# Seven block products for eight: h2 of two token tiles at a time, and a fixed TensorE order in pairs

## The chip, the cores and the metric

The kernel runs on one core of one Trainium2 chip. The metric is device microseconds of one launch. Three runs of the kernel before gave 898.53 us as their median (897.16 to 900.41).

## The reference

Three layers follow each other on 3072 tokens (4 batches of 768). Retention attention gives x (3072 x 512). A first expert part gives y = (h - tanh h) w_out with h = x w_in (inner width 2048). The second expert part, with inner width 1024, is where the change lies:

```python
h = x @ w_in
e = np.exp(h - np.max(h, axis=-1, keepdims=True))
sm = e / (np.sum(e, axis=-1, keepdims=True) + 1e-09)
solu = h * sm
mu = np.mean(solu, axis=-1, keepdims=True)
var = np.mean((solu - mu) ** 2, axis=-1, keepdims=True)
ln = (solu - mu) / np.sqrt(var + 1e-06) * g_ln
return (ln @ w_out).astype(np.float32)
```

Here x is the first part's y. The weights of both parts come as float64 words and are decoded on the chip.

## The kernel before, in words

Engines are named as in the profile: PE is TensorE, DVE is VectorE, ACT is ScalarE, POOL is GpSimd, SP issues most DMAs. A product of two fp32 matrices is made of three matmuls: each operand is split into a high and a low part (a copy to fp32r on ACT, and a subtraction), and high x high, high x low and low x high are added up in PSUM.

The attention is followed by the first expert part, in six column blocks s of 512 tokens. For each f of 16 slices of the inner width, `products_h` (L337) makes 12 matmuls of 128x512 into a PSUM bank, `less_tanh` takes tanh (ACT, L344) and subtracts (DVE, L345), `split` makes the two parts (L350 to L353), and `products_y` (L362) makes 12 matmuls, two f behind. During the last block (s = 5) the weights of the second part are prepared beside this: `dec2.step` loads a weight tile, decodes it (ACT L126, four DVE instructions L133 to L140), scales it if it belongs to `w_out2` (ACT L148) and splits it (ACT L149, DVE L150). That makes 16 weight tiles, 8 of `w_in2` and 8 of `w_out2`. The first y tiles are reloaded from DRAM and split there too (`load_y`, `split_y`: SP L389, ACT L396, POOL L397).

The second part goes over 24 tiles of 128 tokens. `h2(i)` makes 24 matmuls (two halves of 512 columns, four slices of the inner dimension, three matmuls each, L568) into two PSUM banks, then the row maximum (DVE L574), the exponential with its sum (ACT L577), the product h times e with its sum (DVE L579), the subtraction of the mean (DVE L582, result u), the sum of squares (ACT L584) and small instructions that give the scale sc (DVE, POOL L591, L592). `trans(i)` transposes u by 8 matmuls of 128x128 (PE L603) into two PSUM banks, and splits the result (ACT L605, DVE L606). `outp(i)` makes 24 matmuls (L616) and writes the output tile (ACT L619, DMA L621). In the loop, trans runs one tile behind h2, and outp two.

The order of each engine's instructions is found by the framework's scheduler when the kernel is built, from a model of durations. It places instructions of different steps between each other. At run time each engine keeps its order strictly, and waits where an operand is not ready. Buffers come from two pools: `t4` with 44 buffers of 4 KB a partition, and `t2` with 15 of 2 KB.

The change replaces `h2`, `load_y`, `split_y`, the `w_in2` half of `dec2`, and the loop around them.

Of the kernel before, what the change touches and what calls it, by code (L numbers as in the profile page):

```python
# [90 lines left out]
def body(ctx: ExitStack, tc, z, w_in, w_out, w_in2, w_out2, g_ln, cst, tab, out):  # L91
# [274 lines left out]
    def keep_y(s, py):  # L366
# [14 lines left out]
        [w_in2[i] for i in range(NF2)] + [w_out2[i] for i in range(NF2)],  # L381
        [None] * NF2 + [gl[:, i : i + 1] for i in range(NF2)],
        nc.vector,
    )
    yl, ys = {}, {}

    def load_y(i):
        t = t2([P, NK, P], F32, "yl")
        nc.sync.dma_start(out=t, in_=y1d[i // B][:, i % B, :, :])  # L389
        yl[i] = t  # L390

    def split_y(i):
        t = yl.pop(i)
        y = t4([P, 2, NK, P], F32R, "y")
        yh, yo = y[:, 0, :, :], y[:, 1, :, :]
        nc.scalar.copy(yh, t)  # L396
        nc.gpsimd.tensor_tensor(yo, t, yh.bitcast(F32), ALU.subtract)  # L397
        ys[i] = (yh, yo)
# [126 lines left out]
    for n, (s, f) in enumerate(steps):  # L525
# [11 lines left out]
        if s == NSB - 1:  # L537
            if f < NF1 - 3:
                dec2.step()
            if f in (4, 7, 10):  # L540
                dec2.step()
            if f == NF1 - 6:
                load_y(0)
                load_y(1)
            if f == NF1 - 4:
                split_y(0)
# [6 lines left out]
    ps_2 = ctx.enter_context(tc.tile_pool(name="ps_2", bufs=2, space=PSUM, reuse_waits="tile"))  # L553
# [4 lines left out]
    uc, ut, sc2 = {}, {}, {}  # L558

    def h2(i):  # L560
        yh, yo = ys.pop(i)
        ph = ps_2.tile([P, 2, 512], F32, tag="h2", name="ph2")
        for half in range(2):
            n = 0
            for k in range(NK):
                bh, bl = dec2.w[2 * k + half]
                for a, b in ((yh, bh), (yh, bl), (yo, bh)):
                    nc.tensor.matmul(  # L568
                        ph[:, half, :], a[:, k, :], b, start=n == 0, stop=n == 3 * NK - 1
                    )  # L570
                    n += 1
        phf = ph.rearrange("p a b -> p (a b)")
        nmx = sp.tile([P, 1], F32, tag="nmx", name="nmx")
        nc.vector.tensor_reduce(nmx, phf, AX.X, ALU.max, negate=True)  # L574
# [117 lines left out]
```

## Time and profile before

| what | value |
|---|---|
| median of three runs | 898.53 us |
| the profiled execution's own time, as the span from its first to its last instruction | 899.2 us |
| mean granted TensorE clock over the span | 0.988 of full speed |
| busy share of the span: PE, DVE, ACT, POOL | 97%, 48%, 34%, 22% |
| matmuls | 6656 |
| instructions on DVE, ACT, POOL | 873, 606, 200 |

The busy share counts time in which an instruction ran on that engine. Matmuls overlap, so their single durations (some 0.39 us) are longer than the distance at which they follow each other; the pace is read from the starts. In the rows below, "idle before" in square brackets is the time for which the engine stood still ahead of an instruction, and what ended it.

### The profile page before, as it was taken

Reading aid. Unit: us, or ns where it says so; the run is one execution under the profiler, and the core shown is the slowest. Engines: PE = TensorE matmul, PEld = TensorE weight load, DVE = VectorE, ACT = ScalarE, POOL = GpSimd, SP = SyncE. Lnnn points to the kernel's source line nnn. Section 1 sums busy time; section 2 is a strip of 40 time slices with the busy share of each in tenths; the row PEclk is TensorE's granted clock in tenths of the full one; section 3 lists DMA queues with packets and bytes.
Section 4 is the critical chain, followed back from the end, with each engine's and each line's share of the span. In section 5 each row is a group of like instructions: output and inputs, shape, how many; then the busy total and the mean of one; then the engine's idle time right before and its main releaser. Section 6 shows DMA issues by size and latency. Waiting matters only on the chain.

```text
span 899.2 us, 15890 instructions
## 1 busy us (share of the span) xinstructions
PE 874.1 (97%) x6656; PEld 723.5 (80%) x6656; DVE 434.1 (48%) x873; ACT 301.4 (34%) x606; POOL 193.8 (22%) x200
## 2 busy tenths in 40 slices
PE   4699999999999999999999999999999999999998
PEld 4588888888888887888788888888888888888886
DVE  3679759981232232222222279954444444444442
ACT  4556436550111111111111134523444433333332
POOL 4411000000234333333333200011222212122210
PEclk8799999999999999999999999999999999999999
DMA  9663105340321112111310055114111111100000
GB/s 359 251 265 130 48 1 187 95 140 0 94 95 48 60 64 79 48 47 48 95 48 14 12 183 150 43 41 123 47 48 40 35 44 47 36 24 24 24 24 35
DMA packets 34775, 71.93 MB, mean 80 GB/s; under 512 B 3088, under 2 KB 15504, under 8 KB 34704
## 3 DMA queue, kind: packets, MB, share of 16 engines
q1 hardware_dynamic: 18288, 58.01, 19.0%
q10 hardware_dynamic: 16416, 12.91, 4.5%
q8 instruction: 52, 0.85, 0.4%
q14 instruction: 19, 0.16, 0.1%
HBM read 58.32 MB, written 12.58 MB: 79 GB/s over the span
## 4 chain that ended last, share of the span: by engine, by line
PE 94%; DMA 2%; issue 1%; DVE 1%; ACT 1%; POOL 1%; ACTq 0%; POOLq 0%
PE ph L337 29%; PE py L362 29%; PE po L616 15%; PE ph L568 15%; PE out L211 3%; PE ptr L603 2%; PE sc L211 2%; DMA z<-z 1%; DMA con<-cst 1%; DMA y1d<-ysb 0%; POOL qs L223 0%; POOL vs L234 0%; DVE g L345 0%; ACT th L344 0%; DVE w L150 0%
## 5 line engine op out<-in xcount | busy, mean ns | idle before, releaser
L362 PE MATMUL py<-gh,w 128*128 128x512 f32 x768 | 248.8, 392 | 0.0
L337 PE MATMUL ph<-xh,w 128*128 128x512 f32 x768 | 247.9, 393 | 0.0
L337 PEld LDWEIGHTS ph<-xh,w 128*128 128x128 f32 x768 | 145.3, 189 | 31.0
L362 PEld LDWEIGHTS py<-gh,w 128*128 128x128 f32 x768 | 143.3, 188 | 30.4 <-ACT gh L350 0.2
L345 DVE TENSOR_TENSOR g<-ph,th 128x512 f32<-128x512 f32 x96 | 66.2, 690 | 182.3 <-ACT th L344 182.3
L337 PE MATMUL ph<-xl,w 128*128 128x512 f32 x384 | 150.4, 392 | 0.0
L362 PE MATMUL py<-gl,w 128*128 128x512 f32 x384 | 149.8, 390 | 0.0
L344 ACT ACTIVATE th<-ph 128x512 f32<-128x512 f32 x96 | 57.3, 598 | 258.9 <-PE ph L337 245.9
L568 PE MATMUL ph<-w,y 128*128 128x512 f32 x576 | 134.9, 389 | 0.0
L353 POOL TENSOR_TENSOR gl<-g,gh 128x512 fp32r<-128x512 f32 x48 | 61.9, 1289 | 331.6 <-DVE gh L352 298.0
L568 PEld LDWEIGHTS ph<-w,y 128*128 128x128 f32 x576 | 108.0, 188 | 22.4
L616 PE MATMUL po<-w,uh 128*128 128x512 f32 x384 | 120.4, 395 | 0.0
L397 POOL TENSOR_TENSOR y<-yl,y 128x512 fp32r<-128x512 f32 x24 | 42.2, 1761 | 260.9 <-ACT y L396 260.9
L574 DVE TENSOR_REDUCE nmx<-ph 128x1 f32<-128x1024 f32 x24 | 29.4, 1225 | 117.7 <-PE ph L568 117.7
L337 PEld LDWEIGHTS ph<-xl,w 128*128 128x128 f32 x384 | 72.6, 189 | 14.9
L362 PEld LDWEIGHTS py<-gl,w 128*128 128x128 f32 x384 | 72.1, 188 | 14.9
L616 PEld LDWEIGHTS po<-w,uh 128*128 128x128 f32 x384 | 70.6, 188 | 13.6
L616 PE MATMUL po<-w,ul 128*128 128x512 f32 x192 | 75.3, 392 | 0.0
L577 ACT ACTIVATE ex<-ph,nmx 128x1024 f32<-128x1024 f32 x24 | 26.8, 1117 | 132.5 <-DVE nmx L574 132.5
L579 DVE SCALAR_TENSOR_TENSOR ex<-ph,ex 128x1024 f32<-128x1024 f32 x24 | 29.4, 1225 | 29.8 <-ACT ex L577 29.8
L616 PEld LDWEIGHTS po<-w,ul 128*128 128x128 f32 x192 | 36.0, 188 | 7.6
L353 DVE TENSOR_TENSOR gl<-g,gh 128x512 fp32r<-128x512 f32 x48 | 33.8, 707 | 10.1 <-PE py L362 8.1
(76 smaller groups left out, 840.4 us busy)
## 6 DMA issues: line engine op xcount, KB each, us to landing
z<-z SPq DMA_DIRECT2D x48, 512.0 KB, 5.3
raw<-w_in SPq DMA_DIRECT2D x24, 512.0 KB, 5.2
raw<-w_out SPq DMA_DIRECT2D x24, 512.0 KB, 3.7
y1d<-ysb ACTq DMA_DIRECT2D x24, 256.0 KB, 3.5
yl<-y1d SPq DMA_DIRECT2D x24, 256.0 KB, 3.2
out<-ob ACTq DMA_DIRECT2D x24, 256.0 KB, 2.2
tab<-tab SPq DMA_DIRECT2D x5, 256.0 KB, 2.6
tab<-tab ACTq DMA_DIRECT2D x1, 256.0 KB, 4.7
```

Of the source, the lines that this page charges most:

```text
L211: pin(nc.tensor.matmul(o, a, b, start=True, stop=True, skip_group_check=True))
L337: nc.tensor.matmul(ph, a[:, k, :], x, start=n == 0, stop=n == 3 * NK - 1), s < 2
L344: nc.scalar.activation(th, ph, AF.Tanh)
L345: nc.vector.tensor_tensor(g, ph, th, ALU.subtract)
L353: eng_l.tensor_tensor(gl_, g, gh.bitcast(F32), ALU.subtract)
L362: nc.tensor.matmul(py[e], a[:, cols], x, start=f == 0 and n == 0, stop=f == NF1 - 1 and n == 2)
L397: nc.gpsimd.tensor_tensor(yo, t, yh.bitcast(F32), ALU.subtract)
L568: nc.tensor.matmul(ph[:, half, :], a[:, k, :], b, start=n == 0, stop=n == 3 * NK - 1)
L574: nc.vector.tensor_reduce(nmx, phf, AX.X, ALU.max, negate=True)
L577: nc.scalar.activation(ex, phf, AF.Exp, bias=nmx, scale=1.0, accum_out=ssum)
L579: nc.vector.scalar_tensor_tensor(ex, phf, 1.0, ex, ALU.mult, ALU.mult, accum_out=us)
L616: nc.tensor.matmul(po, a[:, f, :], b, start=n == 0, stop=n == 3 * NF2 - 1)
```

## The change

The product of two token tiles with `w_in2` is taken as a 2 by 2 block product. The blocks of the left matrix are A11, A12 (the first tile, first and second half of the 512 inner columns) and A21, A22 (the second tile); the blocks of the right one are B11, B12, B21, B22 (256 inner rows by 512 columns). It is made of seven block products instead of eight: P1 = A11 B11, P2 = A12 B21, and P3 to P7 with sums of blocks on both sides. Each block product is six matmuls (two inner slices, three matmuls each), so a pair takes 42 matmuls for 48.

The weights' side is made once, during the last block of the first part: `Combined` decodes the 8 tiles, forms three sums and one difference a slice on POOL (`combine`, 8 instructions of 128x512 in all) and splits 14 tiles instead of 8. The tokens' side is made for each pair: `split_y(j)` loads two tiles by one DMA, forms four sums on POOL (128x256 each), and splits seven blocks instead of four by three ACT casts (512, 256 and 1024 elements) and three POOL subtractions of the same sizes.

On the output side the PSUM banks of partial results are read and accumulated in steps: P1 is copied out (`keep`, ACT), P6 is accumulated on the same bank and copied out, then P7, copied out again. `add_half` (DVE, one instruction with a running minimum, and a read of it) adds a bank and a copy into `hn` in SBUF and gives the negated maximum, four times a pair. The row maximum of before is gone, and `soft` takes its input from SBUF.

TensorE's order in the second part is the program's order (`manual_schedule`), in pairs; the other engines' order is still the scheduler's.

```diff
+        def combine(self, r):
+            b12, b11, b22, b21 = (self.wf.pop(4 * r + i) for i in range(4))
+            t1, t2_, t4_ = (t2([P, 512], F32, "wf") for _ in range(3))
+            nc.gpsimd.tensor_tensor(t1, b12, b11, sub)
...
+        nc.gpsimd.tensor_tensor(s1, a21, a22, ALU.add)
+        nc.gpsimd.tensor_tensor(s2, s1, a11, ALU.subtract)
+        nc.gpsimd.tensor_tensor(s3, a11, a21, ALU.subtract)
+        nc.gpsimd.tensor_tensor(s4, a12, s2, ALU.subtract)
...
+            nc.scalar.copy(h, src)
+            nc.gpsimd.tensor_tensor(o, src, h.bitcast(F32), ALU.subtract)
...
-            if f < NF1 - 3:
-                dec2.step()
-            if f in (4, 7, 10):
+            if f < 12:
+                com.step()
+            if f >= 8:
                 dec2.step()
...
+    def keep(ph):
+        t = t2([P, 512], F32, "part")
+        nc.scalar.copy(t, ph)
+        return t
...
+        nc.vector.tensor_tensor_reduce(
+            hn[:, half * 512 : (half + 1) * 512], ph, part, -1.0,
+            3.0e38 if seen is None else nm[seen], ALU.add, ALU.min, nm[half],
+        )
...
+    with tc.manual_schedule(engines={mybir.EngineType.PE}):
+        for j in range(NJ + 1):
...
+            if now:
+                h_a, h_b = new_h(), new_h()
+                q1, q2 = bank(), bank()
+                product(j, P1, q1)
+                part1 = keep(q1)
+                product(j, P2, q2)
+                add_half(h_b, 0, q2, part1, None)
+            if was:
+                trans(a)
+            if now:
+                product(j, P6, q1, False)
+                part2 = keep(q1)
+                q3 = bank()
+                product(j, P5, q3)
+            if was:
+                trans(b)
+            if now:
+                product(j, P7, q1, False)
+                part3 = keep(q1)
+                add_half(h_a, 1, q3, part3, None)
+            if was:
+                outp(a, range(4))
+            if now:
+                q4 = bank()
+                product(j, P4, q4)
+                add_half(h_a, 0, q4, part3, 1)
+                soft(2 * j + 1, h_a, 0)
+                product(j, P3, q3, False)
+                add_half(h_b, 1, q3, part2, 0)
+                soft(2 * j, h_b, 1)
+                ys.pop(j)
+            if was:
+                outp(a, range(4, NF2))
+                outp(b, range(NF2))
```

In a pair, a is the second tile and b the first. The new lines that the prediction speaks of are L457 to L460 (sums of a pair, POOL), L468 and L469 (its splits, ACT and POOL), L642 (block products), L649 (keep), L657 (add_half), L667 to L673 (soft), L692 to L695 (trans), L706 (outp) and L712 (the output copy).

Three places show what moved. The first is ACT in the middle of the second part. Before, for one tile (`y` is the split tile, `u` the centred tile, `ob` the output tile):

```order
L577 ACTIVATE ex,ssum<-ph_6738,nmx 128x1024
L605 CAST uh<-ptr 128x512 x2
L396 CAST y<-yl 128x512
L584 ACTIVATE ex,ssq<-u 128x1024
L619 ACTIVATE ob<-po,sc 128x512
L621 DMA out<-ob 128x512
```

Now, for one pair, from its exponentials to the first copy (`part`) of the next pair and the casts of the transposed tiles (`yha` and `yhs` are the high parts of the pair after next):

```order
L667 ACTIVATE ex,ssum<-hn,nm 128x1024 x2
L468 CAST yha<-yl 128x512
L468 CAST yha<-yl 128x256
L712 ACTIVATE ob<-po,sc 128x512
L714 DMA out<-ob 128x512
L673 ACTIVATE ex,ssq<-hn 128x1024 x2
L468 CAST yhs<-ysum 128x1024
L712 ACTIVATE ob<-po,sc 128x512
L714 DMA out<-ob 128x512
L649 COPY part<-ph_6730 128x512
L694 CAST uh<-ptr 128x512 x2
L649 COPY part<-ph_6730 128x512
```

The copies that free a bank for the next accumulation stand behind both sums of squares, a cast and an output copy of the pair before.

The second place is PE where the second part starts. Before, h2 of the second tile is followed by a part of the third, and then by the first transposes (`u_6192` is the first tile's):

```order
L568 MATMUL ph2_6208<-w_5471,y_6154 128x512 x3
L568 MATMUL ph2_6208<-w_5563,y_6154 128x512 x3
L568 MATMUL ph2_6208<-w_5618,y_6154 128x512 x3
L568 MATMUL ph2_6208<-w_5706,y_6154 128x512 x3
L568 MATMUL ph2_6273<-w_5415,y_6203 128x512 x2
L603 MATMUL ptr_6254<-ident_6150,u_6192 128x128 x4
L603 MATMUL ptr_6261<-ident_6150,u_6192 128x128 x4
L568 MATMUL ph2_6273<-w_5415,y_6203 128x512
```

Now the last block product of the first pair (P3, on `ph2_6246`) is followed by P1 and P2 of the second pair, and then by the transposes of tile a of the first (`hn_6215`):

```order
L642 MATMUL ph2_6246<-w_5941,yhs_6004 128x512 x2
L642 MATMUL ph2_6246<-w_5941,yls_6005 128x512
L642 MATMUL ph2_6332<-w_5594,yha_6199 128x512 x2
L642 MATMUL ph2_6332<-w_5594,yla_6200 128x512
L642 MATMUL ph2_6332<-w_5774,yha_6199 128x512 x2
L642 MATMUL ph2_6332<-w_5774,yla_6200 128x512
L642 MATMUL ph2_6333<-w_5597,yha_6199 128x512 x2
L642 MATMUL ph2_6333<-w_5597,yla_6200 128x512
L642 MATMUL ph2_6333<-w_5777,yha_6199 128x512 x2
L642 MATMUL ph2_6333<-w_5777,yla_6200 128x512
L692 MATMUL ptr_6351<-ident_6192,hn_6215 128x128 x4
L692 MATMUL ptr_6358<-ident_6192,hn_6215 128x128 x4
```

Between the end of a tile's h2 and its transposes stood 26 matmuls; now 18 stand between P4, the last product that tile a needs, and its transposes.

The third place is PE at the end. Before, the last tile's transposes (`u_8250`) stand between the matmuls of the output product of the tile before it:

```order
L616 MATMUL po_8321<-w_5897,uh_8261 128x512 x2
L603 MATMUL ptr_8314<-ident_6150,u_8250 128x128 x4
L616 MATMUL po_8321<-w_5897,ul_8262 128x512
L616 MATMUL po_8321<-w_5909,uh_8261 128x512 x2
L616 MATMUL po_8321<-w_5909,ul_8262 128x512
```

Now the transposes of both last tiles stand behind each other, with no matmul between:

```order
L706 MATMUL po_8451<-w_6135,uh_8351 128x512 x2
L706 MATMUL po_8451<-w_6135,ul_8352 128x512
L692 MATMUL ptr_8481<-ident_6192,hn_8297 128x128 x4
L692 MATMUL ptr_8488<-ident_6192,hn_8297 128x128 x4
L692 MATMUL ptr_8497<-ident_6192,hn_8300 128x128 x4
L692 MATMUL ptr_8504<-ident_6192,hn_8300 128x128 x4
L706 MATMUL po_8511<-w_5800,uh_8479 128x512 x2
```

There are two PSUM banks for transposed halves, so the third group of four waits until the first bank has been read.

## Rows read from the trace of the kernel before

**Rows 1.** The page's chain that ended last, by engine and by line.

```profile
PE 94%; DMA 2%; issue 1%; DVE 1%; ACT 1%; POOL 1%; ACTq 0%; POOLq 0%
PE ph L337 29%; PE py L362 29%; PE po L616 15%; PE ph L568 15%; PE out L211 3%; PE ptr L603 2%; PE sc L211 2%; DMA z<-z 1%; DMA con<-cst 1%; DMA y1d<-ysb 0%; POOL qs L223 0%; POOL vs L234 0%; DVE g L345 0%; ACT th L344 0%; DVE w L150 0%
```

**Rows 2.** Busy time by stage (us of PE, PEld, DVE, ACT, POOL, then clock, DMA).

```profile
540.00:560.00 20.00, 20.00 (x90) 16.57 (x89) 19.35 (x40) 7.68 (x13) 0.00 (x0) 1.00 0.52 160
...
700.00:800.00 100.00, 100.00 (x479) 83.55 (x478) 44.70 (x97) 39.67 (x70) 22.14 (x25) 1.00 0.12 38
```

**Rows 3.** Timeline of PE, one tile of the second part (start us, us).

```profile
647.38 5.61 PE L568 MATMUL ph<-w,y 128*128 128x512 f32 x24
652.83 1.03 PE L603 MATMUL ptr<-ident,u 128*128 128x128 f32 x8
653.62 0.71 PE L616 MATMUL po<-w,uh 128*128 128x512 f32 x2
...
659.15 1.07 PE L568 MATMUL ph<-w,y 128*128 128x512 f32 x4
```

**Rows 4.** Groups by line and form, 640 to 860 us (busy us, mean ns of one).

```profile
L606 DVE TENSOR_TENSOR ul<-ptr,uh 128x512 fp32r<-128x512 f32 x38 | 24.4, 682 | 0.0
...
L605 ACT CAST uh<-ptr 128x512 fp32r<-128x512 f32 x38 | 20.2, 588 | 0.0
L584 ACT ACTIVATE ex<-u 128x1024 f32<-128x1024 f32 x19 | 20.2, 1063 | 15.1 <-DVE u L582 15.1
...
L582 DVE TENSOR_SCALAR u<-ex,us 128x1024 f32<-128x1024 f32 x19 | 14.3, 753 | 0.0
L619 ACT ACTIVATE ob<-po,sc 128x512 f32<-128x512 f32 x19 | 13.1, 688 | 9.7 <-PE po L616 9.7
```

**Rows 5.** One line's instructions on POOL (ns: min/median/max), 256 and 512 elements.

```profile
L324 POOL TENSOR_TENSOR xl<-xf,xh x31: 724/732/794, 20.1 to 516.7; 128x256 fp32r<-128x256 f32 x31
...
L397 POOL TENSOR_TENSOR y<-yl,y x24: 1296/1839/1850, 589.4 to 857.5; 128x512 fp32r<-128x512 f32 x24
```

**Rows 6.** Timeline of DVE and ACT, one tile's softmax: where each hop starts.

```profile
700.18 1.23 DVE L574 TENSOR_REDUCE nmx<-ph 128x1 f32<-128x1024 f32 x1 [5.41 <-PE ph L568]
...
702.68 1.23 DVE L579 SCALAR_TENSOR_TENSOR ex<-ph,ex 128x1024 f32<-128x1024 f32 x1 [1.27 <-ACT ex L577]
...
704.14 0.75 DVE L582 TENSOR_SCALAR u<-ex,us 128x1024 f32<-128x1024 f32 x1
...
701.44 1.12 ACT L577 ACTIVATE ex<-ph,nmx 128x1024 f32<-128x1024 f32 x1 [5.96 <-DVE nmx L574]
```

**Rows 7.** Timeline where POOL and DVE meet, 589 and 704 us.

```profile
589.38 2.80 POOL L397 TENSOR_TENSOR y<-yl,y 128x512 fp32r<-128x512 f32 x2 [66.42 <-ACT y L396]
589.51 1.52 DVE L352 CAST gh<-g 128x512 fp32r<-128x512 f32 x1
...
704.21 1.85 POOL L397 TENSOR_TENSOR y<-yl,y 128x512 fp32r<-128x512 f32 x1 [8.53 <-ACT y L396]
```

**Rows 8.** Timeline of PE and ACT where the second part starts.

```profile
612.86 10.59 PE L568 MATMUL ph<-w,y 128*128 128x512 f32 x46
...
612.93 0.59 ACT L372 COPY ysb<-py 128x512 f32<-128x512 f32 x1 [0.65 <-DVE ysb L370]
```

**Rows 9.** Timeline of PE and ACT at the end.

```profile
883.64 0.60 PE L603 MATMUL ptr<-ident,u 128*128 128x128 f32 x4
...
894.80 0.39 PE L616 MATMUL po<-w,ul 128*128 128x512 f32 x1
895.28 0.69 ACT L619 ACTIVATE ob<-po,sc 128x512 f32<-128x512 f32 x1 [4.75 <-PE po L616]
```

**Rows 10.** PE in the attention part: a gap, and the clock after it.

```profile
41.95 0.37 PE L211 MATMUL out<-vq,sa 64*64 64x64 f32 x2 [3.87 <-issue]
...
45.00:50.00 5.00, 5.00 (x76) 3.85 (x75) 1.12 (x3) 1.54 (x4) 2.02 (x2) 0.68 1.03 412
```

More of the change, by code (lines that the diff above doesn't have):

```diff
@@ L380, in body @@
     dec2 = Decoder(
-        [w_in2[i] for i in range(NF2)] + [w_out2[i] for i in range(NF2)],
-        [None] * NF2 + [gl[:, i : i + 1] for i in range(NF2)],
-        nc.vector,
-    )
-    yl, ys = {}, {}
[L387 to L398, printed above, removed]
+        [w_out2[i] for i in range(NF2)], [gl[:, i : i + 1] for i in range(NF2)], nc.vector
+    )
@@ L552, in body @@
     sp = ctx.enter_context(tc.tile_pool(name="sp", bufs=3))
-    ps_2 = ctx.enter_context(tc.tile_pool(name="ps_2", bufs=2, space=PSUM, reuse_waits="tile"))
+    ps_2 = ctx.enter_context(tc.tile_pool(name="ps_2", bufs=4, space=PSUM, reuse_waits="tile"))
     ps_t = ctx.enter_context(tc.tile_pool(name="ps_t", bufs=2, space=PSUM, reuse_waits="tile"))
@@ L557, in body @@
     nc.sync.dma_start(out=ident, in_=cst[:, C_IDENT:])
[L558 to L574, printed above, removed]
+    uc, ut, sc2, po_of = {}, {}, {}, {}
@@ new lines, in bank, with product @@
+    def bank():
+        return ps_2.tile([P, 512], F32, tag="h2", name="ph2")
+    def product(j, m, ph, first=True):
+        a = ys[j][m]
+        n = 0
+        for r in range(2):
+            bh, bl = com.w[m, r]
+            for x, w in ((a[0], bh), (a[0], bl), (a[1], bh)):
+                nc.tensor.matmul(
+                    ph, x[:, r, :], w, start=first and n == 0, stop=n == 5, skip_group_check=True
+                )
+                n += 1
+    def keep(ph):
+        t = t2([P, 512], F32, "part")
+        nc.scalar.copy(t, ph)
+        return t
@@ L575, in h2, with new_h, add_half, soft @@
+    def new_h():
+        return t4([P, FF2], F32, "hn"), [sp.tile([P, 1], F32, tag=f"nm{i}", name="nm") for i in range(2)]
+    def add_half(h, half, ph, part, seen):
+        hn, nm = h
+        nc.vector.tensor_tensor_reduce(
+            hn[:, half * 512 : (half + 1) * 512], ph, part, -1.0,
+            3.0e38 if seen is None else nm[seen], ALU.add, ALU.min, nm[half],
+        )
+    def soft(i, h, last):
+        hn, nmx = h[0], h[1][last]
         ex = t4([P, FF2], F32, "ex")
         ssum = sp.tile([P, 1], F32, tag="ssum", name="ssum")
-        nc.scalar.activation(ex, phf, AF.Exp, bias=nmx, scale=1.0, accum_out=ssum)
+        nc.scalar.activation(ex, hn, AF.Exp, bias=nmx, scale=-1.0, accum_out=ssum)
@@ L592, in h2 @@
         nc.gpsimd.tensor_tensor(sc, sc, ssum, ALU.mult)
-        uc[i], sc2[i] = u, sc
+        uc[i], sc2[i] = hn, sc
     def trans(i):
@@ L607, in trans, with outp @@
         ut[i] = (uh, ul)
-    def outp(i):
-        uh, ul = ut.pop(i)
-        po = ps_o.tile([P, DM], F32, tag="o", name="po")
-        n = 0
-        for f in range(NF2):
-            bh, bl = dec2.w[NF2 + f]
-            for a, b in ((uh, bh), (uh, bl), (ul, bh)):
-                nc.tensor.matmul(po, a[:, f, :], b, start=n == 0, stop=n == 3 * NF2 - 1)
-                n += 1
+    def outp(i, fs):
+        uh, ul = ut[i]
+        if fs[0] == 0:
+            po_of[i] = ps_o.tile([P, DM], F32, tag="o", name="po")
+        po = po_of[i]
+        for f in fs:
+            bh, bl = dec2.w[f]
+            for n, (a, b) in enumerate(((uh, bh), (uh, bl), (ul, bh))):
+                nc.tensor.matmul(
+                    po, a[:, f, :], b, start=f == 0 and n == 0, stop=f == NF2 - 1 and n == 2
+                )
+        if fs[-1] < NF2 - 1:
+            return
         ob = t2([P, DM], F32, "ob")
```

101 lines of the change are left out of this document (81 added, 20 removed).

## The prediction

> **What bounds the kernel now.** I read the chain of waits first: PE is 94% of it, and the second part's two matmul lines, L568 and L616, are 15% of the span each [rows 1]. Then busy time by stage: from 700 to 800 us PE is busy throughout at full clock, DVE for 45%, ACT for 40%, POOL for 22% [rows 2]. So the second part is bound by PE alone, and there removed matmuls shorten the span one for one, as long as PE's fixed order never waits. The timeline of one tile gives the pace: 24 matmuls of h2 take 652.83 - 647.38 = 5.45 us, 0.227 each; the transposes take 0.79; the output product 5.53 [rows 3]. All times below are against the profiled execution's span, 899.2 us; the median of the runs is 0.67 below it, and I take that off at the end. 0.3% (2.7 us) is about what a measurement of this kernel can tell from no change.
>
> **What goes.** 576 matmuls of h2 become 504: 72 x 0.227 = **16.35 us**. Their shape stays, 128x512, so the pace does. The transposes and the output product are the same in number.
>
> **What is added, in the middle of the second part.** All of it lies on engines that idle for more than half of this stage; the question is whether PE's order meets a result that is late. I follow one pair from the end of P4 (0). PE then has P3 (1.36), 36 output matmuls (8.18, to 9.54), P1 and P2 of the next pair (to 12.27), the transposes of a (to 13.06), and P6, which must wait for the copy of P1's bank. Hops are from the trace: PE to a reader 0.25 (the last matmul starts at 894.80, its reader at 895.28, less 0.23) [rows 9]; exponential to product 1.24, product start to centring start 1.46 with its small instructions [rows 6].
> - `add_half` is in no row. Bounds: 0.68 (DVE, 512 elements, one operand in PSUM, L606 [rows 4]) and 1.23 (the reduction of 1024 [rows 6]). I take 0.7, as its size is L606's.
> - So tile a has its maximum at 1.05, exponential to 2.2, product to 3.5; tile b's product runs from 3.65 to 4.9; centring a to 6.0, b to 6.8; squares (1.06 each, L584, and 0.1 for a hop) to 7.2 and 8.35; the cast yhs of 1024 elements (taken as the square's 1.06 [rows 4]) to 9.4; the output copy of b, 0.69, to 10.5, as its product ends at 9.54; the copy of P1's bank (0.59, L605) follows P1's end at 10.9 and is done at 11.8. P6 is due at 13.06. Spare: 1.2 us, and the late part of the chain (the cast's end) could slip by 2.2.
> - The transposes of a need centring a (6.0) at 12.27. P7 needs P6's copy: done 0.84 after P6, with P5 and a transpose (2.15) in between. P3 needs P7's copy and an `add_half`, 1.6 after P7, with 12 output matmuls and P4 (4.1) as cover. None waits.
> - POOL: 256 elements take 0.73, 512 take 1.29 alone [rows 5]; 1024 are in no row, 2.4 by these two. A pair has 5 x 0.73 + 1.29 + 2.4 = 7.35 us for 22, and is split a whole pair ahead. The two `yla` subtractions and the last sum fall behind the cast of `yha`, that is at 4.4, into DVE's chain.
>
> There the two engines meet. A DVE cast of 0.43 that started 0.13 after a POOL instruction took 1.52, and POOL's subtraction of 1.29 took 1.85 when DVE's centring had started just before [rows 7]: whichever was second stood still. So each of DVE's three big instructions there can be held by one POOL instruction: centring b moves from 6.8 to 8.3, the cast's end from 9.4 to 10.5, the copy's hardly at all. Still no wait on PE. The Trainium skill (SBUF — State Buffer, section Who interferes with whom) states it as an exclusive lock, taken for a whole instruction, between GpSimd and a DVE instruction with two SBUF inputs or in a two-port mode. By that rule this change adds to it, because L669 now reads both inputs from SBUF, where L579 had one in PSUM; the trace agrees for the cast (1.52 for 0.43). By the rows' three instructions the sum below stands; by the rule at its strictest, with every POOL instruction of the pair in DVE's way, it would be rival 1's.
>
> **Where PE does wait: the first pair.** Nothing of an earlier pair covers it, and before nothing waited there: 46 matmuls run from 612.86 without a gap [rows 8]. In time after the last y product of the first part (612.86):
> - P1's rest and P2 end at 1.8. P1's copy stands on ACT behind the y copies (to 613.52 [rows 8]) and the 1024 cast of the second pair: done at 0.66 + 1.06 + 0.59 = 2.3, with the hop to PE 2.5. **0.7.**
> - P3 needs 1.6 + 0.1 after P7, covered by P4 alone (1.36). **0.35.**
> - The transposes of a: from P7's end, copy 0.84, two `add_half` 1.4, exponential 1.3, the products of a and b 2.5, small instructions and hops 0.8, centring 0.75: 7.6. PE has P4, P3, P1 and P2 of the second pair and the wait before: 5.8. So 1.8, and 3.1 if one POOL subtraction of 1.29 is in front. I take **2.5.**
> - The transposes of b need the banks of a's. ACT's order in this one pair puts a's casts behind both squares, the 1024 cast and P6's copy: from centring a, 1.1 + 1.2 + 1.1 + 0.6 + 1.2 for the casts + 0.7 + 0.1 for the last subtraction = 6.0; PE has transposes, P6 and P5, 3.5, and the halves overlap by 0.3. **2.2.**
>
> Sum 5.8. Bounds: 4 if POOL is never in front, 8 if `add_half` takes 1.23 and POOL is in front twice.
>
> **And at the end.** Before, the last transposes lie between output matmuls [rows 9]. Now four groups of four stand together on two banks: output copy 0.94, casts 0.59 twice, subtractions to 2.85, the last group to 3.35, where 1.58 would do: **1.8** (bounds 1 and 2.5).
>
> **In the last block of the first part** DVE gets 6 more splits of 0.68 (L606's form), 4.1 us, and POOL 8 instructions of 1.29. DVE is at 19.35 of 20 us there [rows 2], but y products run two f behind, some 10.9 us, and the decoding of `w_out2` moves to where DVE is idle. I cost it at nothing; the cover is that lag.
>
> **Sum:** -16.35 + 5.8 + 1.8 = -8.75: span 890.45, time **889.8**.
>
> **Rivals.**
> 1. *POOL holds DVE for longer* (slower than before). Place: between centring and the cast yhs of each pair. The cast's end at 9.4 may slip by 2.2 for nothing; behind that each us is paid 11 times; the gain is gone at 3.0. If the 1024 subtraction falls in as well, each holding DVE as in [rows 7], it is held for 1.29 + 2 x 0.73 + 2.4 = 5.15: 2.95 x 11 = 32 us, time 922. Against: the order puts that subtraction behind the pair's scale, so after the squares. 7%.
> 2. *`add_half` takes 1.23.* Then the chain is 1.1 longer a pair, with POOL's delay just at its spare, and the first pair pays 1.1 more: 891 to 897, as waits of 0 to 0.5 a pair come in. 11%.
> 3. *The clock falls in the first pair's gaps.* After a gap of 3.87 us the granted clock was 0.68 of 2.4 GHz, a mix of its levels 1.2 and 2.4, for the next stretch [rows 10]. Mine are 2 to 3 us. Some 10 us at two thirds cost 3.5: time 893.3. 9%.
> 4. *DVE is late in the last block of the first part.* If POOL's 8 instructions hold it for their 10.3 us on top of 4.1, and 6 of these are not covered: 896. 6%.
> 5. *The scheduler's order is kept better than I think and the first pair costs under 3 us:* time under 887, at the least 898.5 - 16.35 = 882. 5%.
>
> **Numbers.** Forecast 62%, its own range 886 to 893 by the bounds of the first pair and the end. Range 884.5 to 896.5: forecast, rivals 3 and 5 for the most part, 2 but its end, and half of 4. Faster (under 895.8): forecast 62, rival 2 most 8, rival 3 9, rival 5 5, less 2 for unknown waits, 82%; slower (over 901.2): rival 1 and 1 for the unknown, 8%; same 10%.
>
> **What would show it.** Right: 6584 matmuls; the second part's pairs 22.1 us apart with no gap of PE; some 6 us of PE's idle time within 25 us behind the first P1, put down to ACT or DVE, and 2 us before the last two output products. Wrong: a wait at L642 or L692 in every pair (then the chain through L673, L468 and L649 is longer than 13 us), L657 over 1 us, PE waiting at L362 between 520 and 612 us, or a clock under 1.0 after 612 us.

## The result, and the profile after

The changed kernel takes **890.09 us** (median of 4 runs, 889.34 to 890.77) beside 898.72 for the kernel before (897.16 to 900.41): a ratio of 0.9895, with a 95% interval of 0.9874 to 0.9917. The prediction was 889.8. A second set of runs gave 892.03, a ratio of 0.9912 (0.9898 to 0.9927).

The profiled execution's span is 889.0 us against 899.2. Its page begins like this (busy us, share of the span, instructions), and its chain that ended last reads, against [rows 1]:

```profile
PE 859.5 (97%) x6584; PEld 709.5 (80%) x6584; DVE 464.2 (52%) x951; ACT 335.1 (38%) x660; POOL 278.9 (31%) x268
...
PE 83%; DVE 8%; DMA 3%; issue 2%; ACT 1%; POOL 1%; ACTq 0%; POOLq 0%; DVEq 0%; SPq 0%
```

The 72 matmuls are gone (6656 to 6584), and DVE has come into the chain, with 8%. Busy time by stage, against [rows 2]:

```profile
700.00:800.00 100.00, 100.00 (x477) 83.41 (x476) 53.45 (x130) 52.02 (x90) 41.27 (x45) 1.00 0.13 48
```

The second part is still bound by PE alone: 100 of 100 us at full clock, while POOL's load has nearly doubled (22.14 to 41.27). What PE waited for behind the attention part, in the list of waits (us in total, times, longest):

```profile
PE ptr L692 <- DVE us L670: 2.3, 1, 2.3
PE ptr L692 <- DVE ul L695: 2.3, 2, 1.2
...
PE py L362 <- DVE gh L352: 1.1, 1, 1.1
...
PE ph L642 <- ACT part L649: 0.3, 1, 0.3
```

Four of these five waits are of the second part: three in the first pair, one at the end. The other, at L362, lies in the last block of the first part. PE's timeline has them in brackets:

```profile
601.63 0.39 PE L337 MATMUL ph<-xh,w 128*128 128x512 f32 x1
...
605.84 1.19 PE L362 MATMUL py<-gh,w 128*128 128x512 f32 x4 [1.11 <-DVE gh L352]
...
612.62 0.39 PE L642 MATMUL ph<-w,yha 128*128 128x512 f32 x1
...
614.92 0.73 PE L642 MATMUL ph<-w,yhs 128*128 128x512 f32 x2 [0.32 <-ACT part L649]
...
620.71 0.73 PE L642 MATMUL ph<-w,yhs 128*128 128x512 f32 x2
...
627.42 1.09 PE L692 MATMUL ptr<-ident,hn 128*128 128x128 f32 x8 [2.34 <-DVE us L670]
632.43 1.26 PE L692 MATMUL ptr<-ident,hn 128*128 128x128 f32 x8 [1.15 <-DVE ul L695]
...
870.74 1.03 PE L692 MATMUL ptr<-ident,hn 128*128 128x128 f32 x8
872.93 1.25 PE L692 MATMUL ptr<-ident,hn 128*128 128x128 f32 x8 [1.16 <-DVE ul L695]
873.94 0.70 PE L706 MATMUL po<-w,uh 128*128 128x512 f32 x2
```

What a wait costs is more than its bracket, since PE also has to run its pipeline empty and fill it again. So I count from start to start, at 0.227 a matmul and 0.79 for eight transposes [rows 3]: 0.48 before P6 (at 614.92), 0.34 before P3 (620.71), 2.62 before the transposes of a, 1.50 before those of b, and at the end 873.94 - 870.74 - 1.58 = 1.62. Together 6.6 us. The stretch from the last y product of the first part to the last output copy shrank from 895.28 - 612.86 = 282.42 us [rows 8, 9] to 885.21 - 612.62 = 272.59: 9.8 us, and 16.35 - 6.6 = 9.75. Nothing is left over there.

The wait at L362 (a y product, released by `gh`, the high part that DVE casts) is counted in the same way: from the first part's last h product (L337) to P1's rest (four of its matmuls stand before the last y product, as four of h2's did) 10.99 us pass (601.63 to 612.62), where the kernel before took 9.29 with the same matmuls (603.57 to 612.86). So it costs 1.7, and the change as a whole -16.35 + 6.6 + 1.7 = -8.1 us. That P1 still started 0.2 earlier than h2 is chance: by 490 us this execution was already 1.9 us ahead; its mean granted clock over the first 50 us was 0.90, that of before 0.80. In the 12 other profiles below, the matmul behind the wait at L362 starts anywhere from 603.75 to 607.66 us, in the same kernel too. So beside the ratios I use a **stretch** that leaves the start out: from that matmul to the last output copy, in each kernel's profiled execution. It is 885.21 - 605.84 = 279.37 us here. It comes from one execution, and two of the same kernel differ by 0.56 and 0.11 us in the table. It also leaves out the wait at L362 itself, which is 1.1 us in all runs but three: 4.07 with more POOL, 1.67 with POOL in pieces, 1.66 with all three edits.

### The profile page after: what moved, and what is told of

It is laid out like the page before. It is cut to its first block, busy times and chain, and to the rows that moved or that the text cites. A ratio compares the mean times of both kernels' runs of the same rounds, so it can differ in the third digit from the quotient of the medians.

```text
span 889.0 us, 15985 instructions
## 1 busy us (share of the span) xinstructions
PE 859.5 (97%) x6584; PEld 709.5 (80%) x6584; DVE 464.2 (52%) x951; ACT 335.1 (38%) x660; POOL 278.9 (31%) x268
## 4 chain that ended last, share of the span: by engine, by line
PE 83%; DVE 8%; DMA 3%; issue 2%; ACT 1%; POOL 1%; ACTq 0%; POOLq 0%; DVEq 0%; SPq 0%
PE ph L337 25%; PE py L362 25%; PE po L706 14%; PE ph L642 12%; PE out L211 2%; PE ptr L692 2%; PE sc L211 2%; DVE w L150 2%; DMA z<-z 1%; DVE g L345 1%; DVE wf L137 1%; DVE wf L140 1%; DVE gl L353 1%; DVE gh L352 1%; DVE wf L133 1%
## 5 line engine op out<-in xcount | busy, mean ns | idle before, releaser
L362 PE MATMUL py<-gh,w 128*128 128x512 f32 x768 | 249.2, 392 | 1.1 <-DVE gh L352 1.1
L337 PE MATMUL ph<-xh,w 128*128 128x512 f32 x768 | 247.6, 392 | 0.0
L337 PEld LDWEIGHTS ph<-xh,w 128*128 128x128 f32 x768 | 145.0, 189 | 30.8
L362 PEld LDWEIGHTS py<-gh,w 128*128 128x128 f32 x768 | 143.4, 188 | 31.8 <-DVE gh L352 1.5
L337 PE MATMUL ph<-xl,w 128*128 128x512 f32 x384 | 150.1, 391 | 0.0
L362 PE MATMUL py<-gl,w 128*128 128x512 f32 x384 | 149.9, 390 | 0.0
L706 PE MATMUL po<-w,uh 128*128 128x512 f32 x384 | 118.4, 390 | 0.0
L337 PEld LDWEIGHTS ph<-xl,w 128*128 128x128 f32 x384 | 72.4, 189 | 14.9
L362 PEld LDWEIGHTS py<-gl,w 128*128 128x128 f32 x384 | 72.1, 188 | 15.2 <-DVE gl L353 0.4
L706 PEld LDWEIGHTS po<-w,uh 128*128 128x128 f32 x384 | 72.0, 188 | 15.0
L706 PE MATMUL po<-w,ul 128*128 128x512 f32 x192 | 74.8, 389 | 0.0
L469 POOL TENSOR_TENSOR yla<-yl,yha 128x512 fp32r<-128x512 f32 (+1 forms) x24 | 36.3, 1534 | 114.2 <-ACT yha L468 114.2
L642 PE MATMUL ph<-w,yhs 128*128 128x512 f32 x192 | 61.4, 401 | 0.4 <-ACT part L649 0.3
L667 ACT ACTIVATE ex<-hn,nm 128x1024 f32<-128x1024 f32 x24 | 27.7, 1154 | 51.4 <-DVE nm L657 51.4
L695 DVE TENSOR_TENSOR ul<-ptr,uh 128x512 fp32r<-128x512 f32 x48 | 30.9, 686 | 30.6 <-ACT uh L694 29.7
L149 ACT CAST w<-wf 128x512 fp32r<-128x512 f32 x54 | 32.6, 619 | 31.8 <-DVE wf L140 31.6
L642 PE MATMUL ph<-w,yha 128*128 128x512 f32 x144 | 44.5, 389 | 0.0
L150 DVE TENSOR_TENSOR w<-wf,w 128x512 fp32r<-128x512 f32 x54 | 41.4, 776 | 3.5 <-ACT w L149 3.0
L706 PEld LDWEIGHTS po<-w,ul 128*128 128x128 f32 x192 | 36.0, 188 | 7.7
```

The source lines that it names most:

```text
L149: pin(nc.scalar.copy(hi, wf), fixed)
L150: pin(eng.tensor_tensor(lo, wf, hi.bitcast(F32), ALU.subtract), fixed)
L337: nc.tensor.matmul(ph, a[:, k, :], x, start=n == 0, stop=n == 3 * NK - 1), s < 2
L362: nc.tensor.matmul(py[e], a[:, cols], x, start=f == 0 and n == 0, stop=f == NF1 - 1 and n == 2)
L469: nc.gpsimd.tensor_tensor(o, src, h.bitcast(F32), ALU.subtract)
L642: nc.tensor.matmul(ph, x[:, r, :], w, start=first and n == 0, stop=n == 5, skip_group_check=True)
```

## The experiments

| Kernel | median us | ratio to before, 95% interval | stretch us | to the changed kernel |
|---|---|---|---|---|
| changed kernel | 890.09 | 0.9895 (0.9874 to 0.9917) | 279.37 | |
| the same again | 892.03 | 0.9912 (0.9898 to 0.9927) | 279.93 | +0.56 |
| P4 twice | 907.67 | 1.0091 (1.0074 to 1.0109) | 296.28 | +16.91 |
| scheduler's order | 889.96 | 0.9897 (0.9877 to 0.9916) | 278.49 | -0.88 |
| first pair, first try | 892.75 | 0.9934 (0.9915 to 0.9954) | 280.02 | +0.65 |
| first pair, second try | 889.35 | 0.9863 (0.9838 to 0.9889) | 276.98 | -2.39 |
| last pair | 890.18 | 0.9899 (0.9882 to 0.9915) | 277.90 | -1.47 |
| both, two sets of runs | 888.01, 885.25 | 0.9862 (0.9844 to 0.9880), 0.9854 (0.9837 to 0.9872) | 275.47, 275.36 | -3.90, -4.01 |
| four more copies | 907.04 | 1.0073 (1.0049 to 1.0097) | 296.25 | +16.88 |
| more POOL | 902.62 | 1.0028 (1.0014 to 1.0043) | 288.70 | +9.33 |
| POOL in pieces | 892.19 | 0.9913 (0.9896 to 0.9930) | 280.28 | +0.91 |
| all three | 889.11 | 0.9884 (0.9868 to 0.9899) | 276.22 | -3.15 |

**Is the second part paced by PE's matmuls and nothing else?** P4 twice puts the 72 back:

```diff
+                product(j, P4, q4)
                 product(j, P4, q4)
```

> P4 of every pair is computed twice into the same bank (the second time overwrites the first), which puts the 72 matmuls back and moves nothing else; the result does not change. Theory A (the second part is bound by PE alone, so a matmul is worth its 0.227 us): 72 x 0.227 = 16.35 us more than the changed kernel, less about 0.5 us, as the doubled P4 covers P3's wait of 0.2 and a little of the first transposes' wait in the first pair: 890.1 + 15.9 = 906.0 us, pairs 22.22 + 1.36 = 23.58 us apart. So with eight products in this order the kernel would be 7 us slower than before, which is what the first pair and the end cost. Rival B (a part of the 16.35 is not PE's own: the pairs are paced by a chain through ACT, DVE or POOL that ends nearly with PE's work): part of the added work is free, under 902 us.

Measured: +16.9 us in the stretch and 0.0196 in the ratio, and the pairs stand 677.94 - 654.36 = 23.58 us apart, as theory A has it: 22.22 and 1.36. Rival B falls. The 1 us above the expected 15.9 I put down to the clock (busy us of PE, PEld, DVE, ACT, POOL, then clock, in steps of 2 us):

```profile
626.00:628.00 2.00, 0.00 (x0) 0.00 (x0) 2.00 (x7) 0.56 (x2) 2.00 (x2) 1.00 0.00 0
628.00:630.00 2.00, 1.75 (x9) 1.75 (x9) 1.76 (x5) 1.77 (x3) 1.97 (x3) 0.51 0.00 0
630.00:632.00 2.00, 2.00 (x8) 1.62 (x7) 1.03 (x4) 1.45 (x3) 1.61 (x4) 0.64 0.00 0
632.00:634.00 2.00, 1.60 (x8) 0.97 (x6) 0.56 (x1) 1.56 (x3) 2.00 (x2) 1.00 0.00 0
```

PE stood still from 625.9 to 628.25, and then had 0.51 and 0.64 of 2.4 GHz (1.2 is its lower level) for 4 us. The changed kernel's second profile, whose clock fell at the same place (below), has a stretch of 279.93: against that, P4 twice costs 16.35. So with eight products this order of work would be about 1% slower than the kernel before; the seven products pay for it.

**How much spare has a steady pair?** The copy of P1's bank, which P6 waits for, and P6, in a steady pair of the changed kernel:

```profile
648.53 0.61 PE L642 MATMUL ph<-w,yha 128*128 128x512 f32 x2
...
652.05 0.71 PE L642 MATMUL ph<-w,yhs 128*128 128x512 f32 x2
...
650.09 0.59 ACT L649 COPY part<-ph 128x512 f32<-128x512 f32 x1 [0.59 <-PE ph L642]
```

P1 starts at 648.53, its copy ends at 650.68, P6 starts at 652.05. I put four more copies ahead of it:

```diff
+                for _ in range(4):
+                    nc.scalar.copy(extra, q1)
                 part1 = keep(q1)
```

> P1's bank is copied four times more into a buffer that nothing reads, ahead of the copy that P6 waits for; the result does not change. In the changed kernel that copy ends 1.37 us before P6 begins, and copies that follow each other take 0.49 each. Theory A (that is the pair's whole spare, and behind it each us is paid in each of 11 pairs): 4 x 0.49 - 1.37 = 0.6 us a pair, a wait at L642 (put down to the copy) in every pair of 0.6, 6.6 us in all, 896.7. Rival B (there is more spare, since ACT could begin earlier than the trace shows): under 891.5. Rival C (ACT's casts of the transposes behind it are late too, so that the transposes of b wait as well): 1 us or more a pair, over 901.

Measured: a wait put down to the copy in every pair, as theory A says, but 1.06 us longer pairs (23.28) instead of 0.6, and +16.9 us in all. The four copies took 2.44 together, 0.61 each; the 0.49 I had taken is from casts that overlap (two of 0.59 in 1.07), and these, into one buffer, don't (that the buffer is the reason was not tried). And 2.44 - 1.37 = 1.07: the spare itself was right. The time is that of rival C (over 901), but not by its mechanism: the transposes of b wait in no pair, only in the last turn, as before. Eleven pairs make 11.7 us, the first pair's wait for the copy grew from 0.32 to 2.66, and most of the rest I put down to the clock again: behind that wait and behind the 2.32 before the transposes of a it fell to 0.50, for some 5 and 8 us. The first of these, in steps of 2 us as above:

```profile
616.00:618.00 2.00, 0.00 (x0) 0.00 (x0) 0.00 (x0) 1.91 (x5) 2.00 (x2) 1.00 1.00 287
618.00:620.00 2.00, 1.57 (x6) 1.31 (x7) 0.70 (x2) 0.37 (x1) 2.00 (x3) 0.89 0.05 15
620.00:622.00 2.00, 2.00 (x6) 1.52 (x6) 0.00 (x0) 0.59 (x1) 0.05 (x1) 0.50 0.00 0
```

**Does POOL hold DVE (rival 1)?** Three more POOL instructions amid DVE's centring:

```diff
-        nc.gpsimd.tensor_tensor(s4, a12, s2, ALU.subtract)
...
+            if n == 4:
+                for _ in range(3):
+                    nc.gpsimd.tensor_tensor(s4, a12, ya[0][:, 1, :, :].bitcast(F32), ALU.subtract)
+                nc.gpsimd.tensor_tensor(s4, a12, s2, ALU.subtract)
```

> Three more POOL instructions of 256 elements a pair, written where the last sum goes and overwritten by it, behind the cast yha, so amid DVE's centring and in front of the last sum; the result does not change. By the changed kernel's rows a pair's last sum would end 3.1 us later (3 x 0.74, and the scale's small instructions now ahead of it), the cast yhs 2 us later than now, and the copy of P1's bank some 0.4 us behind P6's due time. Theory A (DVE and POOL hold each other for one instruction at a time, and the chain POOL sum, cast yhs, copy of P1's bank has some 1.5 to 2 us of spare): waits of 0.3 to 0.9 us a pair at L642, 893.5 to 900 us; the two centring instructions of a pair take no longer than their 1.5 and 1.2 and are not held by each POOL instruction in turn. Rival 1 of the prediction (POOL holds DVE for all of its instructions there): centring takes over 2 us each, the transposes of a or the maxima of the next tiles come late too, over 3 us a pair, over 920 us. Rival B: no wait, 890 us.

Measured: +9.3 us in the stretch and, with the longer wait at L362 in front of it (4.07 for 1.11), 12.3 in all; by the ratios it is 12. So the time, 902.62, lies above theory A's 893.5 to 900, and little of it where a theory had put it. In the steady pairs the cast yhs (the high parts of the four sums) does wait for POOL (1.14), and P1's copy ends at 682.70, just when P6 is due; a pair grows from 22.22 to 22.42. The two centring instructions (DVE L674 here) take what they took in the changed kernel:

```profile
674.59 1.52 DVE L674 TENSOR_SCALAR hn<-ex,us 128x1024 f32<-128x1024 f32 x1
...
676.11 1.16 DVE L674 TENSOR_SCALAR hn<-ex,us 128x1024 f32<-128x1024 f32 x1
...
681.17 1.05 ACT L471 CAST yhs<-ysum 128x1024 fp32r<-128x1024 f32 x1 [1.14 <-POOL ysum L469]
682.12 0.58 ACT L652 COPY part<-ph 128x512 f32<-128x512 f32 x1
...
682.75 0.72 PE L645 MATMUL ph<-w,yhs 128*128 128x512 f32 x2
```

Of the three added instructions only one began while the two centrings ran (675.52), the others came behind them; but POOL was busy without a break from 673.75 to 678.57, through both. So rival 1 falls: a centring instruction of 0.75 [rows 4] meets one POOL instruction and then runs. Eleven times 0.2 are 2.2; the rest of the 9.3 us lies at the start: a wait of 3.4 before the transposes of b in the first pair instead of 1.15, one of 1.2 before P6 instead of 0.32, and the clock at 0.50 for some 4 us behind the first of these and for 6 behind a wait of 4.07 at L362. That wait led to the next question.

**Why does PE wait at L362?** There, in the last block of the first part, I had costed DVE's splits and POOL's work at nothing. The changed kernel's timelines of POOL, ACT and DVE:

```profile
576.40 6.56 POOL L457 TENSOR_TENSOR ysum<-yl 128x256 f32<-128x256 f32 x1 [7.81 <-DVE wf L140]
582.92 4.66 POOL L459 TENSOR_TENSOR ysum<-yl 128x256 f32<-128x256 f32 x1
...
597.95 1.06 ACT L468 CAST yhs<-ysum 128x1024 fp32r<-128x1024 f32 x1 [2.53 <-POOL ysum L460]
...
598.91 0.61 ACT L149 CAST w<-wf 128x512 fp32r<-128x512 f32 x1
...
600.46 0.62 ACT L149 CAST w<-wf 128x512 fp32r<-128x512 f32 x1
...
599.59 2.90 DVE L150 TENSOR_TENSOR w<-wf,w 128x512 fp32r<-128x512 f32 x1
...
602.41 1.23 DVE L150 TENSOR_TENSOR w<-wf,w 128x512 fp32r<-128x512 f32 x1
```

DVE is busy for 20.00 of 20 us from 580 to 600 (13.61 before). A POOL sum of 256 elements, 0.73 alone [rows 5], took 6.56 us there. Then ACT stood for 2.53 at the cast yhs, and then two DVE splits of 0.68 took 4.04 together (2.90 and 1.23) while POOL's subtraction and the next sums ran. Which of the two made PE late? I cut pair 0's subtractions into pieces of 256, so that POOL holds DVE for less at a time:

```diff
-            nc.gpsimd.tensor_tensor(o, src, h.bitcast(F32), ALU.subtract)
+            step = 256 if j == 0 else n * 256
+            for c in range(0, n * 256, step):
+                nc.gpsimd.tensor_tensor(
+                    o[:, c : c + step], src[:, c : c + step], h[:, c : c + step].bitcast(F32), ALU.subtract
+                )
```

> Pair 0's POOL subtractions, that run in the last block of the first part, are cut into pieces of 256 elements; nothing else changes. In the changed kernel two DVE splits of 0.68 took 4.04 us there while POOL's subtraction of 1024 took 2.86, and PE then waited 1.11 us at L362. Theory A (POOL and DVE hold each other for one instruction, so that DVE gets its turn between two pieces): the two splits take under 3 us, PE's wait at L362 goes, 1.1 us faster. Rival B (the engine that is let in is POOL again, or the wait comes from DVE's own 20 of 20 us of work): the splits still take 4 us or the wait stays at 1 us.

Measured, in the same timelines of POOL, ACT, DVE and PE:

```profile
592.16 6.70 POOL L471 TENSOR_TENSOR yla<-yl,yha 128x256 fp32r<-128x256 f32 x3 [1.07 <-ACT yha L468]
...
599.59 1.05 ACT L468 CAST yhs<-ysum 128x1024 fp32r<-128x1024 f32 x1 [4.67 <-POOL ysum L460]
...
601.19 0.82 DVE L150 TENSOR_TENSOR w<-wf,w 128x512 fp32r<-128x512 f32 x1 [3.62 <-ACT w L149]
602.47 0.69 DVE L150 TENSOR_TENSOR w<-wf,w 128x512 fp32r<-128x512 f32 x1 [0.46 <-ACT w L149]
...
605.89 1.20 PE L362 MATMUL py<-gh,w 128*128 128x512 f32 x4 [1.67 <-DVE gh L352]
607.63 0.50 PE L362 MATMUL py<-gl,w 128*128 128x512 f32 x1 [0.54 <-DVE gl L353]
```

The splits are down to 0.82 and 0.69, so POOL no longer holds DVE there, as theory A had it; and PE's wait, for `gh` and then for the low part `gl`, has **doubled**, from 1.11 to 1.67 and 0.54. The 1.1 us that theory A expected to gain did not come: 0.9913 beside 0.9912 for the changed kernel on the same chip. So the hold is not the only thing that makes PE late. What grew is ACT's wait for POOL's last sum (2.53 to 4.67): three pieces took 6.70 where the two instructions had taken 4.38. By my reading each piece has to get past DVE anew, since DVE's instructions beside them kept their usual lengths (0.41 to 0.68). The links, in the order of the rows: DVE, busy without a break, starves POOL; POOL's sum is late; ACT stands at the cast yhs, with the casts of the splits (L149) behind it; DVE stands at the splits, for ACT (3.62 idle here) or held by POOL's subtraction (4.04 in the changed kernel); and the cast gh of the next f, that PE's y product needs, is behind them on DVE. In the changed kernel itself the rows put the 1.1 us on the hold: the casts of the two splits had ended at 599.52 and 601.08, before the splits began (599.59 and 602.41), and DVE did not stand still before either. Had the second split begun at 601.08, gh would have ended at some 603.4 by the distances of the rows and without a further hold (an estimate), before PE was due at 604.58. With pieces, ACT's link alone makes PE wait. No run takes away both. The wait of 4.07 with more POOL begins with another link: ACT stood 5.36 us for a decoding instruction of DVE (L140), which had taken 1.23 for 0.68 beside POOL's added instructions, as the one before it had (1.22), and then the cast yhs did not have to wait for POOL.

**What is the fixed order worth?** Without it:

```diff
-    with tc.manual_schedule(engines={mybir.EngineType.PE}):
+    if True:
```

> The seven products stay; TensorE's order of the second expert part is left to the scheduler. Theory A (the fixed order loses some 4.5 us in the first pair and 1.6 at the end, since nothing stands ready to fill the waits, and nothing in the pairs between): the scheduler's order brings products P1, P2, P5 and P6 of the second pair forward, so the first pair loses under 2 us, and the time is 885 to 888 us, if its order meets no late result in the ten pairs between. Rival B: its order was made with durations that differ from the chip's, and PE waits for transposes or copies in many pairs: over 893 us.

Measured: 0.9897, so the fixed order makes no difference that these runs can tell; theory A's 885 to 888 was missed, and so was rival B's time of over 893. The scheduler takes P1, P2, P5 and more of the second pair forward, and no transposes wait any more. But it also puts output matmuls early, and they wait for ACT's casts (uh, the high parts of the transposed tiles); from its list of waits:

```profile
PE po L706 <- ACT uh L694: 2.6, 3, 1.6
```

**Can the first pair's loss be filled?** In the second pair's turn alone (j = 1), PE's order becomes P1, P2, P5, P6, P4, trans(a), P7, trans(b), outp(a, 0 to 3), P3, the rest:

> In the second pair's turn alone PE's order is P1, P2, P5, P6, P4, transposes of a, P7, transposes of b, half of a's output product, P3, the rest; the sums of the third pair are put behind it. All that it moves ahead of the transposes depends on nothing of the first pair. Theory A (the first pair's loss, as read from the changed kernel's waits, is 2.3 us before the transposes of a and 1.2 before those of b, because only P1 and P2 stand ahead of them): the wait before a's transposes goes, P7 waits about 0.5 us for the copy of P6's bank behind the squares, b's transposes about 0.3: 2.7 us faster than the changed kernel, 887.4 us. Rival B: what is lost there is set by DVE's and ACT's chains for the whole pair, so the wait only moves to P7 and P3, and the time stays within 1 us of 890.1.

Measured: +0.65 us in the stretch, and yet half of theory A is right. (By the ratios it is 3.5 us; the profiled execution, 891.81, is 0.9 faster than the median, and the rest is not accounted for.) From 616 to 650 us PE does not wait; then, in the third pair's turn, the timelines of ACT and PE show:

```profile
652.01 1.04 ACT L468 CAST yhs<-ysum 128x1024 fp32r<-128x1024 f32 x1 [1.44 <-POOL ysum L460]
652.96 1.07 ACT L694 CAST uh<-ptr 128x512 fp32r<-128x512 f32 x2
...
654.32 1.97 PE L692 MATMUL ptr<-ident,hn 128*128 128x128 f32 x8 [3.02 <-DVE ul L695]
```

I had put the third pair's sums behind all this, so POOL came late by a pair, and ACT stood at the cast yhs with the transposes' casts behind it. After this wait of 3.02 the clock was 0.55 and 0.60 for 4 us. Second try, with the call of split_y moved forward:

```diff
                 part2 = keep(q1)
+                split_y(j + 1)
```

> The same order of PE in the second pair's turn (P1, P2, P5, P6, P4, transposes of a, P7, transposes of b, half of a's output product, P3, the rest), but the sums of the third pair stand behind P6's copy there, so that ACT has no cast in front of the third pair's transposes that waits for POOL. Theory A (the first pair's loss is a want of ready work in front of its transposes, and what the run with the same PE order lost again 3.0 us later was the cast yhs behind late POOL sums): no wait before the transposes of a, under 1 us before those of b (the cast yhs of 1.05 stands ahead of theirs), none in the pairs behind; the second part takes 3 us less than the changed kernel's 276.4, so 273.4, and the time is some 887. Rival B (the wait moves on whatever the order): a wait of 2 us or more in the second or third pair, time over 889.5.

Measured: -2.39 us in the stretch; the wait before the transposes of a is gone, 1.28 stays before those of b (I had said under 1), and no later pair waits. The waits are a want of ready work, as theory A says. **At the end**, the transposes of the last a go between the parts of the product before, those of b behind it:

```diff
+            outp(b, range(5))
+            trans(2 * j + 1)
+            outp(b, range(5, NF2))
+            trans(2 * j)
```

> The last pair's transposes of a are put between the two parts of the output product of the pair before (behind f = 4), those of b behind that product; nothing else moves. Theory A (the four groups of transposes at the end wait for their two banks to be cast, and lose 1.6 us): PE has no wait there, 888.5 us. Rival B: the transposes of a, now 2 us earlier, meet the centring of a not yet done, or the casts on ACT stand behind the squares and the output copy, so that the wait is only moved: within 0.5 us of 890.1.

Measured: no wait there, -1.47 us in the stretch for 1.5 expected; the ratio, 0.9899, can't tell it from the changed kernel. Then both:

> The order of the second pair's turn of the run before and that of the last pair (transposes of a between the two parts of the output product of the pair before) together. Theory A (the two losses are apart from each other, 3 us and 1.5): the second part takes 271.9 us, time 885.5. Rival B: the spread of the kernel's start, 1 to 1.5 us, hides it, or one of the two comes back as another wait: over 888.

> The changed kernel as it is, beside the others on one chip: by the first result 0.9895 of the kernel before, with the same waits (2.3 and 1.2 us in the first pair, 1.2 at the end, 1.1 at L362). If one of its executions has the lower clock behind the first pair's 2.3 us, as two other kernels had behind gaps of 2.3 and 2.7, it is 1.5 to 2 us slower than the rest.

> The two changed orders (second pair's turn, last pair) together, once more and beside the changed kernel on the same chip. Theory A, by the traces: 3.9 us less in the second part, so 0.0043 under the changed kernel's ratio (0.985). Rival B: the start's spread is what the first comparison shows, and the two are within 1.5 us.

Measured: -3.90 and -4.01 us in the stretch, the sum of the two. Beside the changed kernel on one chip the ratios are 0.9854 (0.9837 to 0.9872) and 0.9912 (0.9898 to 0.9927), intervals that don't touch: **this version beats both kernels**. That is 5.2 us; the stretch shows 3.9 of them, and what the rest is was not shown. Its first median, 888.01, was above the 885.5 expected and just in rival B's range (over 888), its second, 885.25, was not. What PE still waits for behind the attention part, in its list of waits:

```profile
PE ptr L692 <- DVE ul L695: 1.3, 1, 1.3
PE py L362 <- DVE gh L352: 1.1, 1, 1.1
PE ph L642 <- ACT part L649: 0.3, 1, 0.3
```

The changed kernel's second profile shows rival 3 at work (busy time in steps of 2 us again, the clock third from the end), behind the same wait of 2.34 us that had left the clock at 1.00 in the first:

```profile
626.00:628.00 2.00, 1.35 (x10) 1.26 (x11) 1.92 (x5) 1.37 (x3) 2.00 (x3) 0.91 0.00 0
628.00:630.00 2.00, 2.00 (x6) 1.62 (x5) 1.25 (x6) 1.85 (x3) 1.58 (x4) 0.50 0.00 0
630.00:632.00 2.00, 2.00 (x7) 1.29 (x5) 0.53 (x3) 1.57 (x3) 2.00 (x2) 0.74 0.00 0
```

It cost 0.56 us in the stretch, where 1.5 to 2 had been expected, for the slower PE came to the transposes of b when they were nearly ready (a wait of 0.15 instead of 1.15). Last, all three edits, with split_y(j + 1) behind trans(a):

> Both changed orders and the pieces together, and in the second pair's turn the third pair's sums now stand behind the transposes of a, so that ACT casts those before it touches the third pair. Theory A: the wait of 1.28 before the transposes of b goes too, and that of 1.1 at L362: some 6 us less than the changed kernel, 884. Rival B (ACT's cast yhs, that waits for POOL's sums, now holds the transposes' casts of b or the exponentials, as it did in the first try): a wait of 2 us or more in the third pair, within 1.5 us of the run with both orders alone.

Measured: 0.9884, which is neither: theory A's 884 is missed, and the median is 3.9 us above the 885.25 of both orders where rival B allows 1.5. The wait of 1.28 before the transposes of b did go. But by rival B's mechanism ACT stood for 3.47 at the cast yhs, with the casts of b's transposes behind it, and P6 of the third pair waited 1.65 (rival B had said 2 or more); the pieces brought their 2.2 at L362 along.

## Why the prediction was right, and where it was off

- **PE's pace.** Pairs of 22.22 us, 22.1 predicted, without a gap. That each removed matmul is worth 0.227 us is shown by P4 twice.
- **The steady pair.** From P4's end (661.23 in one pair): centring a ends at 6.6 (6.0 predicted), b at 7.8 (6.8, or 8.3 with POOL), the cast yhs at 9.9 (9.4 to 10.5), the copy of P1's bank at 11.7 (11.8), and P6 starts at 13.0 (13.06). `add_half` takes 0.69 where 0.7 was taken (0.75 in its form with a third operand, and 0.08 for a read behind it), so rival 2 with its 1.23 falls. POOL's 1024 elements take 2.40, as estimated. The spare of 1.2 is 1.37, and the run with four copies found its edge there.
- **POOL and DVE.** Each centring is held by one POOL instruction: 0.75 became 1.53 and 1.15 in a steady pair, as [rows 7] had let expect, and no more of POOL's comes in between. The Trainium skill (SBUF — State Buffer, section Who interferes with whom) has this as a lock for a whole instruction. The traces agree where one instruction meets one (DVE's 1.53 for 0.75). POOL's 6.56 for 0.73 at 576 us goes further: no DVE instruction beside it is longer than 0.69, so by this row POOL stood behind several in a row. The strictest reading of the rule, rival 1, does not come about.
- **The first pair.** 0.48, 0.34, 2.62 and 1.50 us, 4.9 in all, for 0.7, 0.35, 2.5 and 2.2, 5.8. The last term was too large by 0.7. That the waits come from a want of ready work is shown by the second try (-2.39).
- **The end.** 1.62 for 1.8, shown by the run that takes it away (-1.47).
- **The step that failed** is "In the last block of the first part ... I cost it at nothing; the cover is that lag". It cost 1.7 us. The cover had been counted against DVE's own 4.1 us. It was not counted against a DVE that leaves POOL no room: a sum of nine times its length, and behind it ACT's queue and then DVE's. It was rival 4's place, and with POOL's hold of the splits a part of its mechanism, at 1.7 of its 6 us. PE waiting at L362 was also one of the prediction's own signs of being wrong, and it came; so the time was right with one of its terms wrong.
- **The clock** (rival 3) is right as a mechanism: it fell in one of the changed kernel's two profiled executions, for 0.56 us, where 3.5 was priced. A clock under 1.0 after 612 us had been another sign of being wrong.

The rows for `add_half`, POOL's 1024 elements and the centring, from the changed kernel: two lines' instructions (ns: min, median, max)

```profile
L657 DVE CUSTOM_DVE_ANT_0 hn<-ph,part x24: 681/692/693, 615.0 to 857.9; 128x512 f32<-128x512 f32 x24
...
L469 POOL TENSOR_TENSOR yls<-ysum,yhs x12: 2366/2401/2858, 599.1 to 826.9; 128x1024 fp32r<-128x1024 f32 x12
```

and the timeline of POOL and DVE where they meet in a steady pair:

```profile
665.48 2.97 POOL L469 TENSOR_TENSOR yla<-yl,yha 128x512 fp32r<-128x512 f32 x2 [11.71 <-ACT yha L468]
...
666.32 1.53 DVE L671 TENSOR_SCALAR hn<-ex,us 128x1024 f32<-128x1024 f32 x1
...
667.84 1.15 DVE L671 TENSOR_SCALAR hn<-ex,us 128x1024 f32<-128x1024 f32 x1
```

So two losses were 0.9 and 0.2 too large, and one of 1.7 was missing: -8.1 by the rows for the -8.75 predicted. That the medians differ by only 0.3 us from the forecast owes something to errors that cancel, and that is luck. How often the clock falls in executions without a profile isn't known, and a split of pair 0 on an engine other than POOL wasn't tried.

## What to carry to other kernels

Fewer matmuls pay one for one where PE is bound, as long as the added work ends before PE's next use of it; count that spare in a steady turn, and then count the first and the last turn by themselves, because nothing of a neighbour covers them. There a loss is a want of ready work, and another order in that one turn gives it back (3.9 of 6.6 us here). Before putting a POOL result into ACT's queue, look at what stands behind it: in four of these runs (first try, more POOL, POOL in pieces, all three) a late POOL sum made PE wait for what stood behind it in that queue.

## What the runs showed of the hardware that was not expected

- A gap of 2.3 us of PE can be followed by the lower clock, or not: at the same place, behind the same wait of 2.34, it stayed at 1.00 in one execution of the changed kernel and fell to 0.50 in another. With a wait of 2.3 there in other kernels it fell in three (P4 twice, four copies, POOL in pieces) and stayed in two (last pair, more POOL). Behind 2.66, 3.02, 3.4 and 4.07 us it fell each time.
- A POOL instruction of 0.73 us took 6.56, 4.66 and 4.04 in a row beside a DVE without idle time, and cutting POOL's work from two pieces to three made it longer in sum (4.38 to 6.70, at much the same place).
